# A planned kernel for a state-space convolution beside a gated feed-forward: another order of the same work

## The chip, the cores and the metric

The kernel runs on one core of a Trainium2 chip. The metric is the device time of one execution in microseconds, given as the median of several runs. A core has TensorE (PE in the profile, with its weight loads as PEld), VectorE (DVE), ScalarE (ACT), GpSimd (POOL) and SyncE (SP), and 16 DMA engines that move what the queues of SP and POOL ask for.

## The reference

```python
def reference(A_u, A_A_re, A_A_im, A_B_re, A_B_im, A_C_re, A_C_im, A_log_dt, A_Dskip, B_x, B_w_gate, B_w_up, B_w_down, gate_w):
    x = A_u                                           # 1 x 2048 x 512
    g = _sigmoid((x * gate_w).sum(-1, keepdims=True))
    a = _A_ref(x, ...)   # K[d,l] = Re sum_n C exp(dt A l) dt B, N = 128; y = causal conv of u with K (by FFT) + u * Dskip
    b = _B_ref(x, ...)   # (sigmoid(x Wgate) * (x Wup)) Wdown, F = 1792
    return g * a + (1 - g) * b
```

All arrays are float32. A is a diagonal complex state-space model per channel (512 channels, 128 states), whose kernel K of 2048 taps is convolved with the input. B is a gated feed-forward of width 1792. A gate per row mixes them.

## The kernel before, in words

**Feed-forward.** The 2048 rows are taken in two halves, each in two blocks of 512 rows; the 1792 hidden columns in 14 slices of 128, in groups of 3, 4, 4 and 3. Each float32 operand is split in a high and a low part (`split`, line 1057 on): a DMA into a staging buffer `st`, a copy on ScalarE, a subtraction on VectorE. A product is three matmuls (high-high, high-low, low-high). `hidden` (matmuls at line 1130, tile `gups`) makes gate and up products; `post` makes the gated hidden tile on ScalarE and VectorE in turn (lines 1173 to 1180); `down` (line 1202, tile `dps`) sums a group's slices for 128 rows in one accumulation bank; `add` scales it by 1 - g and adds it to the output in memory by an accumulating DMA of POOL (line 1226), or, for late rows, into a tile on VectorE (line 1215).

**State-space part.** `steps` computes exp(log_dt) on POOL, stores it (`dts`, line 446) and it is read back to all partitions by `preludes` (lines 468, 469). `powers`, `angles`, `magnitudes` and `tables` (lines 509 to 628) build tables of the powers of exp(dt A) on VectorE and ScalarE; `tables` contracts them over the 128 states on TensorE (line 653, tile `kps`, 16 blocks). `second` applies the first step of a discrete transform (line 683, `wps`, 8 blocks), evicts to `kev` and stores to memory `a_k` (line 698). `rows` does the same for the input (line 742, `ups`, 8 blocks), stored to `a_u` (line 782). `passes` works in two halves j of 256 channels, four steps each: it loads constants `wwu`, `wwk`, `wwv`, the input's part `au` (line 819) and the kernel's part `ak` (line 828); `ustep` transforms au (line 849, `s2u`), `kstep` transforms ak (line 876, `s2k`), `prod` multiplies them on VectorE, `inverse` transforms back (line 914, `ips`), `evict` copies and stores to `b_s` (line 936). `finals` reads `b_s` (line 977), `last` makes the last transform (line 990, `fps`), scales by g and adds to the output.

The matmuls of these steps are small and use the array in pieces (128x32, 32x64, 32x32, 64x32); those of the feed-forward use all of it. s2u, s2k, ips, wps and ups each need both of the two double banks `xb`; fps needs one. In the first half there is one buffer `big` for au and ak in turn; in the second there are three, two of them in space of the tables (in the profile they appear as `parts`).

**The order.** Each part is a generator that yields one step at a time (engine, cost, function, what it waits for). `Plan.run` takes the letters of the string `ORDER` one after another; a letter names a kind of step and an engine, and the first waiting step of that kind on that engine is put out. So ORDER is the program order on every engine, the DMA issues of SP and POOL among them; each engine works its instructions off in that order, and each instruction waits for its data and buffers by semaphores. The costs that steps give are used in `Plan` for times in the plan: with a given ORDER they decide only which of several equal free buffers a step takes, and no instruction. The letters that this text needs:

| letter | step | letter | step |
|---|---|---|---|
| d, e | hidden, down on PE | 5, 9, # | ustep, kstep, inverse on PE |
| Y, p, c, + | tables, second, rows, last on PE | f, $ | loads of passes, of finals, on SP |
| D, E, F | loads of x, of gate and up, of down weights | x, r, ) | stores to a_u, a_k, b_s |
| A, C, L | step sizes, pw table, prelude loads | g, 2 | late output rows (SP), accumulating DMA (POOL) |

Of the kernel before, what the change touches and what calls it, by code (L numbers as in the profile page):

```python
# [66 lines left out]
ORDER = (
    "ABEjDkhidDhEdHGDhjikddEjikIEDjkhddiEjkKZatatatdEdayzjktbFlDhiEjdyzAdkdddDhiEmedjkFydduzDhiLLMlNymMCOOPGDhdiydQOFRSdldmQE"
    "QQbZzezddQOTRyzejQWyddkWTWOWyTEjEzWdEWd0eeeTd1dOPQWEzWcWddjyyyUVVWkW0eeZdejdkvxxxW0exzvcLZx1xzWxaUeeaxzOEdUUyQWUWzFa1dWv"
    "xyQdRSTadWkExxxEyddRWtWX0YTtztQjvzTTUdtbxxxyseexeddQyyOVdVbZdUUzUUkRuj0e1leedScZQXyz0YdWzjTR1WkdseWGnovxedymWzjWeTdyddTk"  # L70
    "LTzdWkWzWWWxyzvyx1EUWEWdz0eedxFxy1xFxcedFZWjVzkWddldmWlmyyVUzUdxalmtUvxxaxx0ejvaxpqdaeeEUzyRSTdxqzje02yEtWddeeeeRTTEtWkd"
    "WWX0Y2tdrybxErTUseeededbMZzVNxMdOO02edejyeeVUPQOkUydUdQzUjRkScXZzEQz0YQQO2dTRseejQWydeneWTrjWWWWdkWdWWzvyzWxyeddzdWTv0ee"
    "eWTWdU1yEzky0eeeecdZOVVxoEWx0eeeeWzddWx2OPQdvjr2kOQQUExFUxly2UUzLRyduxSTFxkvWRmdWpxydadtzWXjkTTzFa0YlmxyTQlxFdylmUtsdzmd"
    "xeeyezadtjVxkQzxyLzeOVUExaEdj0qeUete2Uqer2r0dURyESTeeezyXed0YQb2jksR2dTbWzWedeeeTjZkckWdTy0eeWeWeWvxxxxEdUdV20eeZeexvWrx"
    "xxxWdcWVnW2WW0eejeezyWUUWUU2zWRSdyvx0eeeFFzoTdeWdRFWxlvpmrkdyzWWX2ldDDmD0YTyzTTxl2hdmiqsydehehUdMNizMOOeLxViPQOVUUUUdRSQ"
    "dx0DeQyzQXe2e0QOTRyddYQW2zWWsnodWqxrrrrOWTWyzThWOPWeedQdpWedTiWUxyWWOdqDDxWzWqrrr0edeVeyWzrVUUWUU0ddhyQDhQezdfRSf4566yzW"
    "hTRe2Wdd2e0QidyDhWeXiTieeizdy0YTTUQzfOf89%VVUUUdULdddseeQey2zX0dR%S2u2YdWyzWTRW%sndydW%WETef!EjkWFzeeTd02dTWUWyjWzWkW#&f"
    "ffdW&))))4VddVUWUEUeUWyzeeEdyzWR01e&&))))jdee01W5WfWeeSoe668pd0eeeq1TRWXq9rrEyzdyzk%r0YTT1TUdseyz%MddedV%NeMl%dOVydUjfd!"
    "#ydOPQjdOQQUUUXrzk0kQRSffEQO&YsddQeezWW1edEWWWjkEdWTRyzyjydTWnzd0eeejy&)dGW))WTzWkdzdm4)W0eeefdykWF1TUzOWEyz&dydWFoVWdVU"
    "UUjz&d)51))UOyfz668dRSlmy)lWdpWTdRkdyqqfrWdWzX90FzEY%TTTyzlyU1ddErrjkdyPmmQzseeee%Vd0e2eeeOEz%QVWUUU%!URdQ0e2eeeQXyQOdS0"  # L80
    "z2YTRQWWWWWW#fWWdjkyseeeeWdWEno&rdT&))))WTf40ee2eeTdUWj&k&5)jW)dy0ee2eedVfW))ffVd6zyWWzUU60Uep8UqEqRS2WTedeer9zdWXdRTydy"
    "0TYd%s%e%F%2!kerF#TU((dElm)z)))ydedejkrVzdVzddUUFyUlUXm0j&Y&Eyy))))jlrEdzkEkzmFsnopqqeedd$y$*jrzlmrdrrgy$f$+,*zzfydd-dy-"
    ",zfdzefy,k.z.e,3+--,ee45768g.ffef.e-,,3fE9%%%%ffgjd4d.ededj578e.,kEeyz3,E69%%%edegjff!.%fd.fed#((&ge)&)4k5376e)f)8g)E)f9"
    "yjy)z)k!f%e%edefd2%d3f#(&))&)&)d)ye4)56%e))6jfkd!8#$&&))))ee&()))$)9z3ykee%dd%%dyged%!e#&zzyg$$())))3d(())))ez*ed*+,zy-+"
    ",--zdyde-dFld$-zy--$z--F$dyd*+,dl$d*-d-yF$$--*-,+,..,elzme,..mzym$eeeeeee-z-3$3-e,33+yez,.,.e-ee,--g*--g-gee+3g,..,e-3ee"
    "-3-g--eeeee-g3ge3g")
# [243 lines left out]
def body(ctx, tc, xp, xt, prm, ldt, dsk, gw, wgu, wdn, c_wu, c_wf, c_wk, c_wwk, c_wwu, c_wwv, c_pw, out):  # L330
    nc = tc.nc
# [333 lines left out]
    def second(q, kss, kst, kready):  # L665
# [29 lines left out]
        te = []  # L695
        for x in range(4):
            dst, src = a_k[q // 4][q % 4, x], kev[32 * x:32 * x + 32]
            te.append((yield "SP", kb(215), lambda: S.dma_start(
                dst.rearrange("r l k d -> l r (k d)"), src.rearrange("p (r k) d -> p r (k d)", r=2)), [max(end)]))
# [72 lines left out]
    def urest(t4, e, i, ph, banks, tp):  # L772
        es, = yield EVU, 1
        ev = es.tile("evu")
        te = yield ("ACT", "DVE"), either(2 * D), lambda eng: copy(eng, ev, ph), [tp, es.t]
        banks.free(te)
        done = []
        for r in range(2):
            for h in range(2):
# [2 lines left out]
                done.append((yield "SP", kb(150), lambda: S.dma_start(dst, src), [te]))
# [7 lines left out]
    def passes():  # L790
# [11 lines left out]
        for j in range(NW):  # L802
# [9 lines left out]
            for p2 in range(4):  # L812
# [6 lines left out]
                ta.append((yield "SP", kb(520), lambda: S.dma_start(au.rearrange("p i g d -> p (i g d)"), src), [sa.t, rdone.t]))  # L819
# [8 lines left out]
                tk.append((yield "SP", (kb(740), 0.2), lambda: S.dma_start(ak.rearrange("p o i g d -> p o (i g d)"), src), [sk.t, kdone[j].t]))  # L828
# [34 lines left out]
    def kstep(wks, wwk, sk, ak, ready, both, tk):  # L863
# [6 lines left out]
        def mms():  # L870
            for i in range(2):
                for c in range(2):
                    for g_ in range(4):
                        for r in range(2):
                            q = slice(64 * r, 64 * r + 64)
                            mm(pk[i][32 * g_:32 * g_ + 32, r, c], wwk[q, i, g_, c], ak[q, :, i, g_], start=True, stop=True,  # L876
                               tile_position=(64 * r, 32 * g_), skip_group_check=True)
# [177 lines left out]
    def split(kind, src, hi, lo, slot, ready, n=512):  # L1055
# [4 lines left out]
        t = yield "SP", kb(0.55 * n), lambda: S.dma_start(flat if len(src.shape) == 2 else st, src), [s.t]  # L1060
# [239 lines left out]
```

## Time and profile before

| | |
|---|---|
| median of 3 runs | 615.53 us (615.13 to 615.72) |
| the profiled execution | 617.09 us, of which the span of instructions 615.3 us |
| TensorE clock granted, mean | 0.983 |
| instructions | 16787 |
| matmuls | 7147: 1344 `gups`, 672 `dps`, the rest pieced blocks |
| moved by DMA | 104.19 MB, mean 169 GB/s |

A row of busy time by line names the line, the engine, the operation, what is written and read, the shape and the count, then busy us, mean ns of one, idle time ahead and what ended it. Consecutive matmuls overlap, so the mean of one is longer than the step from one to the next. A row of the timeline has start, duration, engine, line, what is written and read, and the count of instructions merged. A row of PE's waits has us in total, times and the longest. A load's time to landing runs from its issue to its last byte.

### The profile page before, as it was taken

The page shows a single profiled execution, that of the slowest core. Times are in us where ns is not written, and L with a number is a line of the kernel's source. Part 1 is how long each engine was busy: PE and PEld are TensorE (multiplying, and loading weights), DVE is VectorE, ACT ScalarE, POOL GpSimd, SP SyncE. Part 2 cuts the span into 40 slices and gives each one's busy share as a digit, 9 for nine tenths or more (in the row PEclk, how much of TensorE's full clock was granted, in tenths as well). Part 3 has the DMA queues.
Part 4 walks back from the last instruction along what each step waited for, and adds up shares of the span by engine and source line. Part 5 has one row for each costly group of instructions (what it writes and reads, how often), then busy time and mean ns, then how long its engine had stood idle before and what let it go on. Part 6 is the DMA issues. An engine that isn't in the chain of part 4 may idle for free.

```text
span 615.3 us, 16787 instructions
## 1 busy us (share of the span) xinstructions
PE 590.5 (96%) x7147; PEld 453.0 (74%) x7147; DVE 539.9 (88%) x765; ACT 414.8 (67%) x663; POOL 51.2 (8%) x80
## 2 busy tenths in 40 slices
PE   7999999999999999996999999999999988998997
PEld 3777777887778777884787778777777756676775
DVE  3899999999999997996899999999988566867897
ACT  3597979688798767995867878788957432231340
POOL 5000000010101111100110000001110022000031
PEclk7999999999999999997999999999999998999999
DMA  7612807562675586487518725444955799898776
GB/s 224 216 34 74 289 26 215 176 134 35 172 177 142 109 183 154 82 191 221 126 19 242 201 80 167 135 152 54 244 146 137 220 300 315 245 271 264 236 200 164
DMA packets 74156, 104.19 MB, mean 169 GB/s; under 512 B 7009, under 2 KB 45793, under 8 KB 73058
## 3 DMA queue, kind: packets, MB, share of 16 engines
q1 hardware_dynamic: 67170, 92.64, 49.9%
q0 software_dynamic: 6912, 10.49, 12.5%
q8 instruction: 56, 0.92, 0.6%
q14 instruction: 18, 0.15, 0.1%
HBM read 61.15 MB, written 41.95 MB: 168 GB/s over the span
## 4 chain that ended last, share of the span: by engine, by line
PE 75%; DMA 9%; issue 7%; DVE 3%; ACT 2%; SPq 1%; POOL 0%; DVEq 0%; ACTq 0%; POOLq 0%
PE gups L1130 40%; PE dps L1202 20%; PE kps L653 5%; PE s2k L876 3%; DMA ak<-a_k 2%; PE wps L683 2%; PE s2u L849 2%; PE ips L914 2%; PE ups L742 1%; DMA b_s<-ev 1%; DMA out<-part 1%; DMA st<-xt 1%; PE fps L990 1%; DMA wwk<-c_wwk 1%; DMA st<-wdn 1%
## 5 line engine op out<-in xcount | busy, mean ns | idle before, releaser
L1130 PE MATMUL gups<-x,gu 128*128 128x512 f32 x1344 | 334.7, 397 | 2.7 <-ACT x L1063 1.5
L1130 PEld LDWEIGHTS gups<-x,gu 128*128 128x128 f32 x1344 | 252.4, 190 | 69.6 <-issue 9.2
L1202 PE MATMUL dps<-dnw,h 128*128 128x512 f32 x672 | 172.7, 395 | 0.9 <-DVE h L1180 0.9
L1202 PEld LDWEIGHTS dps<-dnw,h 128*128 128x128 f32 x672 | 124.5, 188 | 36.9 <-issue 7.1
L1226 POOL DMA_DIRECT2D out<-part x32 | 28.3, 885 | 421.4 <-ACT part L1221 286.4
L581 ACT ACTIVATE B<-B 128x32 f32<-128x32 f32 (+2 forms) x96 | 53.9, 676 | 0.3
L1221 ACT ACTIVATE part<-dps,omg 128x512 f32<-128x512 f32 x48 | 32.8, 682 | 27.6 <-PE dps L1202 26.9
L1175 DVE SCALAR_TENSOR_TENSOR sg<-sg,gups 128x512 f32<-128x512 f32 x56 | 37.8, 680 | 9.8 <-ACT sg L1173 5.9
L1173 ACT ACTIVATE sg<-gups 128x512 f32<-128x512 f32 x56 | 33.0, 590 | 14.7 <-PE gups L1130 13.7
L1179 ACT ACTIVATE h<-sg 128x512 fp32r<-128x512 f32 x56 | 34.6, 622 | 11.3 <-DVE sg L1175 11.3
L609 DVE TENSOR_TENSOR t<-T,bz 128x1024 f32<-128x1024 f32 (+3 forms) x48 | 41.2, 859 | 0.6
L611 DVE TENSOR_TENSOR T<-T,t 128x1024 f32<-128x1024 f32 (+3 forms) x48 | 41.4, 863 | 0.3
L610 DVE TENSOR_TENSOR T<-T,bz 128x1024 f32<-128x1024 f32 (+3 forms) x48 | 41.3, 861 | 0.0
L1180 DVE TENSOR_TENSOR h<-sg,h 128x512 fp32r<-128x512 f32 x56 | 38.2, 685 | 2.5 <-ACT h L1179 2.4
L1064 DVE TENSOR_TENSOR gu<-st,gu 128x512 fp32r<-128x512 f32 (+1 forms) x50 | 32.9, 663 | 7.0 <-ACT gu L1063 7.0
L1063 ACT ACTIVATE gu<-st 128x512 fp32r<-128x512 f32 (+1 forms) x50 | 30.3, 607 | 12.0 <-DMA st<-wgu 11.9
L653 PEld LDWEIGHTS kps<-B,T 128*32 128x32 f32 x2048 | 29.9, 110 | 9.3 <-issue 6.7
L653 PE MATMUL kps<-B,T 128*32 128x64 f32 x2048 | 33.0, 220 | 2.1 <-issue 2.1
L355 ACT ACTIVATE ev<-ips 128x512 f32<-128x512 f32 x23 | 13.0, 594 | 30.9 <-PE ips L914 17.1
L499 ACT ACT_TABLE_LOAD x21 | 26.9, 1283 | 0.3
L692 ACT ACTIVATE kev<-wps 128x1024 f32<-128x1024 f32 x16 | 15.8, 1024 | 13.5 <-PE wps L683 13.3
L575 DVE TENSOR_TENSOR B<-pp,pw 128x1024 f32<-128x1024 f32 x16 | 19.6, 1224 | 4.9 <-PE kps L653 4.8
(124 smaller groups left out, 698.6 us busy)
## 6 DMA issues: line engine op xcount, KB each, us to landing
st<-wgu SPq DMA_DIRECT2D x46, 256.0 KB, 4.7
a_u<-evu SPq DMA_DIRECT2D x64, 128.0 KB, 3.8
a_k<-kev SPq DMA_DIRECT2D x32, 256.0 KB, 3.7
out<-part POOLq DMA_DIRECT2D x32, 256.0 KB, 4.7
b_s<-ev SPq DMA_DIRECT2D x64, 128.0 KB, 3.1
st<-wdn SPq DMA_DIRECT2D x25, 256.0 KB, 3.8
ak<-a_k SPq DMA_DIRECT2D x5, 1024.0 KB, 7.1
parts<-b_s SPq DMA_DIRECT2D x10, 512.0 KB, 6.1
```

The costliest lines, as they stand in the source:

```text
L581: A.activation(B[:, :, 0, 1 << k::2 << k], B[:, :, 0, 1:64 >> k:2], AF.Exp, scale=float(1 << k))
L609: yield "DVE", c, lambda: V.tensor_tensor(t2, src, sb, op=OP.mult), [t, slot.t]
L610: te = yield "DVE", c, lambda: V.tensor_tensor(dst, src, br, op=OP.mult), [t]
L611: te = yield "DVE", c, lambda: V.tensor_tensor(dst, dst, t2[:, :, ::-1], op=OP.add), [te]
L653: mm(p[32 * jj:32 * jj + 32, s], T[:, 32 * i + ch, c], B[:, ch, c], start=(c == 0), stop=(c == 1), tile_position=(0, 32 * jj), skip_group_ ...
L1064: te = yield "DVE", dve(n), lambda: V.tensor_tensor(lo, st, hi.bitcast(F32), op=OP.subtract), [te]
L1130: mm(p, gu[:, a, k, dc], x[:, b, dc], start=(dc + n == 0), stop=(dc == NC - 1 and n == 2))
L1173: t = yield "ACT", actp(512), lambda: A.activation(sg, pg_, AF.Tanh, scale=0.5), [tg, ss.t]
L1175: t = yield "DVE", dve(512), lambda: V.scalar_tensor_tensor(sg, sg, 1.0, pu, op0=OP.add, op1=OP.mult), [t, tu]
L1179: t = yield "ACT", act(512), lambda: A.activation(h[:, 0], sg, AF.Copy), [t, hs.t]
L1180: t = yield "DVE", dve(512), lambda: V.tensor_tensor(h[:, 1], sg, h[:, 0].bitcast(F32), op=OP.subtract), [t]
L1202: mm(p, h[:, a, 128 * s:128 * s + 128], dn[:, b], start=(f == fs[0] and n == 0), stop=(f == fs[-1] and n == 2))
```

## The change

The string ORDER is replaced by another of the same 2178 letters' length. The count of each letter is the same but for four kinds: evictions of the inverse on ScalarE 23 to 20 and on VectorE 9 to 12, steps of `last` on ScalarE 22 to 23 and on VectorE 34 to 33 (steps that may run on either). Beside it, cost figures that the planner uses are edited: TensorE's cost of a change of array shape, and the sizes that stand for the rate of single transfers. No instruction's shape or operand is edited.

```diff
 ORDER = (
-    "ABEjDkhidDhEdHGDhjikddEjikIEDjkhddiEjkKZatatatdEdayzjktbFlDhiEjdyzAdkdddDhiEmedjkFydduzDhiLLMlNymMCOOPGDhdiydQOFRSdldmQE"
...
+    "kABEjDkhiddEjkEjDkhiHIEjDhGiddddKZEjatDhiddatkddEjkatatbEyddDjkhEDyddjzkddhizAyuFlyzDhmizdiDhLLidydeMNzdddGyFMyddCOOPlmQ"
...
-            c = n + (0.0 if mode == self.last else 0.09 if self.last == "f" else 0.21 if mode == "f" else 0.1)
+            c = n + (0.0 if mode == self.last else 0.18 if self.last == "f" else 0.33 if mode == "f" else 0.2)
...
-        t = yield "PE", ("f", 0.95, 4), lambda: mm(p[:, 0], warm[:1, :P], row, start=True, stop=True), [t, bank.t]
+        t = yield "PE", ("f", 1.95, 4), lambda: mm(p[:, 0], warm[:1, :P], row, start=True, stop=True), [t, bank.t]
...
-            te.append((yield "SP", kb(215), lambda: S.dma_start(       # a_k
+            te.append((yield "SP", kb(295), lambda: S.dma_start(
...
-                ta.append((yield "SP", kb(520), lambda: S.dma_start(au...
+                ta.append((yield "SP", kb(1010), lambda: S.dma_start(au...
...
-                tk.append((yield "SP", (kb(740), 0.2), lambda: S.dma_start(ak...
+                tk.append((yield "SP", (kb(1130), 0.2), lambda: S.dma_start(ak...
```

The other edits are of the same kind: stores to a_u and b_s 150 to 139, s2k 1.57 to 1.68 us, loads of b_s 540 to 485, accumulating stores 215 to 230, staging loads 0.55 to 0.52 per column.

The PE letters of the two strings, from the first c on, around the places that the prediction speaks of (p is the fourth and the eighth, 5 and 9 the first and the fifth; the last row is from the fifth 5 to the last #):

```
before  p e d d e d e e d d e d 5          after  p d e d e d d d e d d e e d e 5
before  p e e d d d + d d d d e e + e e 5 e e 9
after   p d d d d d d d d d + + d d d e 5 d e e 9
before  5ee9ddeded5ee9ededed#e5e9eededd#de5ed#ee9eedddede#
after   5dee9edeeded59eededed#eeee59ededee#eed5ee#d9deeededd#
```

And the SP letters around the first load of a_u (x is the last of its 64, r the last four of the first 16, f the loads of passes):

```
before  D D x r r r r D f f D f f
after   D D r x r r r f f f D D f
```

From the first of the loads of passes in the second half on, the SP letters are (g late output rows):

```
before  f $ f f f g f f f f E f f g E E g f f f f g ) ) ) f ) g ) E ) f ) )
after   f f f f g f f f f f f g E f f f f g ) ) f ) ) E ) f f g E ) ) ) f f
```

More of the change, by code (lines that the diff above doesn't have):

```diff
@@ L72 @@
[L72 to L83, printed above, removed]
@@ L84 @@
-    "yjy)z)k!f%e%edefd2%d3f#(&))&)&)d)ye4)56%e))6jfkd!8#$&&))))ee&()))$)9z3ykee%dd%%dyged%!e#&zzyg$$())))3d(())))ez*ed*+,zy-+"
-    ",--zdyde-dFld$-zy--$z--F$dyd*+,dl$d*-d-yF$$--*-,+,..,elzme,..mzym$eeeeeee-z-3$3-e,33+yez,.,.e-ee,--g*--g-gee+3g,..,e-3ee"
-    "-3-g--eeeee-g3ge3g")
+    "kABEjkDhiddEjkEjDkhiHIEjDhGiddddKZEjatDhiddatkddEjkatatbEyddDjkhEDyddjzkddhizAyuFlyzDhmizdiDhLLidydeMNzdddGyFMyddCOOPlmQ"
+    "OQzRSzeddEbZQTQRQOjkQWEEFlcZmeyTyEdWWzWdzWdjkWOTWyOEWPF0eeeyTvxxxxWzWdU1EjkvxxxxWQddyWzW0ee1eddcOWWzVWQWdVUWUdUEUElyjkWj"
@@ new lines @@
+    "RyvxxxSk0e1ZeXaatxaeddazjQyjvxxxxGjQd01YTRdyseeezddtztTddTzkTUkdtEQObVyVUUULdUu0ee1yzbyzRSeZXd0dyQYcWWjseedeWvxxZdzddWzd"
+    "WTRdWykmzyvWnWydxTTT0eeFWxEFxzlWkcdyZaledWWUVzVddxdWLmFmWzx1ExWa0yUzUljmeyvxxeetkzUdxWUxWRSeEa02aydvxxxxee1opejedTqdWtRW"
+    "Xy02YTdzdtTEktbseedeTUebMqdVNEzMOO02dVUeeedeyZPQOjkyUjyddQUUXrRzQ0Y2QckSZr1QOseeeezTznddREjvxxrxQWxWWWryydd0eeee2TzzdWTW"
+    "WkWWdTOvxxWWUEyxWzOcxPW0eyzeee2WWdVyVU0dedFdevFQUjkydUZal2xxOQaEazEjQWkdtyeeddvURSxFoxTQpzddjzRTWkWjWXkTamxxExF0Yd2yzyTz"
@@ new lines @@
+    "tUQylmseezOdldmeVlmyzVe0deeeExeUQuUUUEXRyt0dzSjY2k2dTERtWWbWbZseWWqeeneqrTWrrrjW0deTjeedyzcZ2TvxxxLkxUWWe0WdWeedeevcxWWy"
+    "xVk2zxVd0eeeexUU2UURSjkvxxyxvop0eeeeqWdTRyz0eeeFlFzdedLxddxDxWmFTlWmWTWyT2WDX0YDyzzhiDhiyhdsedeqlrhrUzMNmedViMLOOPQiddOV"
+    "UU2Ur0eeeUXQyQd0QzxrR2QOdSYyzTedRseenQWWopdOWWOWWy2zTTWPWW0e2dedTdDdUdeyqqzW2VDrxWWWrydrzQOrfff4dVUUUDhiyzQ0eedeQDyUWzW0"
+    "yhRSWW56fTedheeddRWhdQi6WiTzX80Yyzi9TdTUy22dsezQV%%VUUUUXOdyzee0ydQRSdY2sWd%eee0dyneefWTEWj%!#WEFdzjWkRWl2fde&dWzWdd&))E"
@@ new lines @@
+    "))fWkTWTmW0TUW4Eoedyzj&&)yde5VkzWWW)VUULUf)y1UeWzdu0e16yzedRSe6p0feedeE8jykEWdqT12RWWXqr9r0YdzTddTT%ydUjjV%MNsdeVEjeeyd%"
+    "dz)MOOUPQOyfdedQyUQUURXd10Y%Q!#rfQOSTRsde1eQE&Wz&TWf4WnzdzWdkWTyWdWzW))TU0eeedWyzkr)1ydzdVWOdyWVWUU)&&5E)of0edefUjUkFk6y"
+    "F)6)1zpq)8WRWSTWddydREq9rzWWTjkWOfdeWldzdlXPmd%T0YQOjyzyrzydzdmQTUFdyseeeEzlme%V02VQdee1Qkee02Qjy%dU%!UUeUkRSeeXOEze0dYT"
+    "RQWWW2#seeEyjfzWkWdedWWnWW&&))))TyTWdWf4TUW&e0WrdEezedoW&)))5)fjreeVWVUUUU60eeeWy6pRjqqeWdSWTyRf89%%W%d20eTeeedX2T0Y2TUs"
@@ new lines @@
+    "%dy#df!Vkze&zG2EredVydeedkrFlr())U)y)UUUX0YF(dEr&)))mj)lskzemnopEjkFdFE$zyq$*qrlddyzrddjrzydkdyddzzr$mz$*+,-gf+,-,,f4-yz"
+    "dfddeyzy5f..,,lgzy668fmzfdee39-,,%%%f4efjdfeedeyfgd..573%kE.689%.,,.%efedededy!f4.%#3ee&e%(zefy(jf(g576893ez))kf%de!)%%)"
+    "dE)jkeffe4g3E)#()e&e)fdf()))jf)(k%57e!)6e)zy))#E8(gdgy$&)2())&)$9)j3kdee)e)d%)ed%dy%g$$%!#*z&()))d&z)dy())))3eeeFe*zFz+y"
+    "F3+,zlld-dy--d$,d--me$-d-$*+,---dy-dd--$*l$-+$*,,zy$+$*.med.,me,,dzzeee--y3eee.yee,ezze.,+e-yz.3e-3.,,-3-g.--gg-g,-3-eee"
@@ L88 @@
+    "3--.eg--gee3geee3g")
 XLATE = 0
@@ L781, in urest @@
                 src = ev[64 * r + 32 * h:64 * r + 32 * h + 32].rearrange("p j (w d) -> p (j w) d", w=NW)
-                done.append((yield "SP", kb(150), lambda: S.dma_start(dst, src), [te]))
+                done.append((yield "SP", kb(139), lambda: S.dma_start(dst, src), [te]))
         es.free(max(done))
@@ L818, in passes @@
                 src = a_u.rearrange("r s e j w g d -> w (r s e j) g d")[j][:, 8 * p2:8 * p2 + 8].rearrange("x g d -> x (g d)")
-                ta.append((yield "SP", kb(520), lambda: S.dma_start(au.rearrange("p i g d -> p (i g d)"), src), [sa.t, rdone.t]))
+                ta.append((yield "SP", kb(1010), lambda: S.dma_start(au.rearrange("p i g d -> p (i g d)"), src), [sa.t, rdone.t]))
                 ready, both = [Ev(), None], Ev(2)
@@ L827, in passes @@
                 src = a_k[j].rearrange("o x r l (c p y) d -> p (r l c) (o x) (y d)", c=2, p=4)[p2]
-                tk.append((yield "SP", (kb(740), 0.2), lambda: S.dma_start(ak.rearrange("p o i g d -> p o (i g d)"), src), [sk.t, kdone[j].t]))
+                tk.append((yield "SP", (kb(1130), 0.2), lambda: S.dma_start(ak.rearrange("p o i g d -> p o (i g d)"), src), [sk.t, kdone[j].t]))
                 plan.spawn(kstep(wks, wwk, sk, ak, ready, both, max(tk)), "kstep")
@@ L877, in mms @@
                                tile_position=(64 * r, 32 * g_), skip_group_check=True)
-        t = yield "PE", ("64x32", 1.57, 129), mms, [tk] + [b.t for b in banks]
+        t = yield "PE", ("64x32", 1.68, 129), mms, [tk] + [b.t for b in banks]
         sk.free(t)
@@ L935, in evict @@
                 src = ev[64 * r + 32 * c:64 * r + 32 * c + 32]
-                end.append((yield "SP", kb(150), lambda: S.dma_start(dst, src), [max(te)]))
+                end.append((yield "SP", kb(139), lambda: S.dma_start(dst, src), [max(te)]))
         es.free(max(end))
@@ L976, in finals @@
                 src = b_s[j][:, :, q, 4 * t4:4 * t4 + 4].rearrange("c k j d -> (c k) (j d)")
-                tb.append((yield "SP", kb(540), lambda: S.dma_start(b[:, q].rearrange("p j d -> p (j d)"), src), [sb.t, bdone[j].t]))
+                tb.append((yield "SP", kb(485), lambda: S.dma_start(b[:, q].rearrange("p j d -> p (j d)"), src), [sb.t, bdone[j].t]))
             plan.spawn(last(j, t4, b, sb, max(tb)), "last")
@@ L1022, in last @@
                 t = 4 * t4 + k[i]
-                done.append((yield "POOL", kb(215), lambda: nc.gpsimd.dma_start(out[t, :, cols], y[:, i], accum_op=OP.add), [max(t1), begun[t]]))
+                done.append((yield "POOL", kb(230), lambda: nc.gpsimd.dma_start(out[t, :, cols], y[:, i], accum_op=OP.add), [max(t1), begun[t]]))
                 begun[t].set(done[i])
@@ L1059, in split @@
         st = flat if len(hi.shape) == 2 else flat.rearrange("p (a b) -> p a b", a=hi.shape[1])
-        t = yield "SP", kb(0.55 * n), lambda: S.dma_start(flat if len(src.shape) == 2 else st, src), [s.t]
+        t = yield "SP", kb(0.52 * n), lambda: S.dma_start(flat if len(src.shape) == 2 else st, src), [s.t]
         def halves():
```

3 lines of the change are left out of this document (removed).

## The prediction

> **What bounds the kernel now.** I read the page's engine totals first, then busy time by stage, then PE's waits and, where those lie, the timelines of PE and SP and the chain of waits.
>
> ```profile
> span 615.3 us, 16787 instructions
> ```
> ```profile
> PE 590.5 (96%) x7147; PEld 453.0 (74%) x7147; DVE 539.9 (88%) x765; ACT 414.8 (67%) x663; POOL 51.2 (8%) x80
> ```
> ```profile
> 20.00:60.00 40.00, 38.75 (x195) 30.33 (x194) 39.86 (x70) 30.93 (x54) 0.00 (x0) 1.00 0.30 90
> 260.00:300.00 40.00, 34.64 (x466) 27.32 (x458) 32.92 (x46) 30.71 (x47) 3.48 (x4) 0.91 0.76 189
> 500.00:540.00 40.00, 35.98 (x567) 24.02 (x566) 30.36 (x36) 9.60 (x16) 6.62 (x8) 0.96 0.99 279
> ```
>
> The span is 96% TensorE. The stage rows (busy us of PE, PEld, DVE, ACT, POOL, then PE clock, DMA share, GB/s) say where it isn't: 260 to 300 and 500 to 540 lose over 5 and over 4 us of PE and are the rows with a lowered clock. VectorE is a second pacer: 39.86 of 40 us busy in 20 to 60, but only 32.92 in 260 to 300, when TensorE stands still.
>
> ```profile
> PE s2u L849 <- DMA wwk<-c_wwk: 5.4, 1, 5.4
> PE s2k L876 <- DMA ak<-a_k: 2.6, 1, 2.6
> PE kps L653 <- issue: 2.1, 3, 1.4
> PE s2k L876 <- ACT ev L355: 1.7, 1, 1.7
> ```
>
> Two waits for loads of intermediate results stand out. "Issue" waits have no releaser in the trace; a new order can't be shown to remove them, so I leave them in. With the operations unchanged, the new order can only change PE's idle time, the array's changes of shape, and clock lost by idling.
>
> **One: fewer changes of shape.** The PE letters of ORDER, read off, give the sequence of PE steps: 517 in both. The letters d and e use the whole array; Y, p, c, 5, 9, #, + use it in pieces. Changes of shape fall from 121 to 114, stretches of pieced work between whole-array work from 58 to 53.
>
> ```profile
> 565.90 1.36 PE gups L1130 x6
> 567.94 1.43 PE ips L914 x61
> 569.37 1.59 PE gups L1130 x6
> ```
>
> Six whole-array matmuls take 1.36 us (0.227 each), and 1.59 right behind a pieced block. One stretch less so saves about 0.23: five save 1.2 us (ends 0 and 2, if entering a block costs something too).
>
> **Two: the first load of a_u.** SP issues in order.
>
> ```profile
> 268.29 0.44 SPq L782 DMA_DIRECT2D a_u<-evu  x1
> 270.96 2.77 SPq L698 DMA_DIRECT2D a_k<-kev  x4
> 273.83 1.50 SPq L1060 DMA_DIRECT2D st<-xt  x1
> 275.51 1.56 SPq L815 DMA_DIRECT2D wwu<-c_wwu  x1
> 277.13 0.44 SPq L819 DMA_DIRECT2D au<-a_u  x1
> ```
> ```profile
> 266.46 2.10 PE L683 MATMUL wps<-wk,kst 32*64 32x128 f32 x128
> ...
> 285.72 2.37 PE L849 MATMUL s2u<-au,wwu 32*32 32x256 f32 x64 [5.36 <-DMA wwk<-c_wwk]
> ...
> 289.47 2.90 PE L1130 MATMUL gups<-x,gu 128*128 128x512 f32 x8
> ```
> ```profile
> a_u<-evu SPq DMA_DIRECT2D x64, 128.0 KB, 3.8
> ...
> au<-a_u SPq DMA_DIRECT2D x4, 1024.0 KB, 7.2
> ```
>
> PE's clock is the time base. The wps block (letter p, its fourth) starts at 266.46; PE is free for s2u at 285.72 - 5.36 = 280.36, 13.9 us later; the au load, issued 277.13, keeps s2u waiting until 285.72, 19.3 us after wps. (The row names the wwk load, which s2u does not read; of its own inputs au is the late one.) Then 5.36 us of idling cost clock too: eight gups take 2.90 where 8 x 0.227 is 1.8, and the three dps ahead of them are slow alike. With s2u itself slow (2.37, against 1.43 for the ips block of the same shape and count above) the place costs about 5.4 + 0.9 + 1.1 = 7.4 us by these rows, and with 0.5 for the dps 7.9.
>
> In the new order, between the same two blocks stand 9 d and 6 e instead of 6 d and 5 e: 9 x 1.36 + 6 x 0.68 against 6 x 1.36 + 5 x 0.68, so 16.3 against 11.6, 4.8 us more cover; PE reaches s2u 18.7 us after wps. The load's side: SP can issue the first of the four a_k stores 4.5 us after wps (270.96 - 266.46), and the last a_u store now stands behind that one (before, it was ahead, at 268.29): 4.9. It must have landed before au is issued: with the median 3.8 that is 8.7, and with 7.2 for au the data is there at 16, or at 18 if each runs a microsecond over its median. The load of xt that sat ahead of wwu (1.50 us) now comes after. So 18.7 against 16 to 18: no wait, at best by 0.7 us. Bounds: all 7.9 gone, or, if SP gets to that store 5 us late, none. I take 7.0.
>
> What is late next is VectorE.
>
> ```profile
> 70.86 1.21 DVE L611 TENSOR_TENSOR T<-T,t 128x1024 f32<-128x1024 f32 x1
> ```
> ```profile
> 72.75 1.44 PE L653 MATMUL kps<-B,T 128*32 128x64 f32 x88
> ```
> ```profile
> 477.44 1.22 DVE L590 TENSOR_TENSOR B<-B,ex 128x1024 f32<-128x1024 f32 x1
> ```
> ```profile
> 479.27 1.94 PE L653 MATMUL kps<-B,T 128*32 128x64 f32 x124
> ```
>
> These are the first and the last of 16 kps blocks; each starts about 0.6 us after VectorE's last operation on its tables, and 14 of the 16 within 2.3 us. So TensorE can't run ahead of VectorE by more than that, unless VectorE too is freed of idle time. It idles 40 - 32.92 = 7.1 us in the stage of this wait; part of that was waiting on the stalled PE. I give back 2 us (between 0 and 7): net -5.
>
> **Three: the first a_k load of the second half.**
>
> ```profile
> 482.85 1.34 PE wps L683 x77
> 489.75 4.75 DMA a_k<-kev
> 495.41 13.73 DMA ak<-a_k
> 509.27 3.21 PE s2k L876 x64
> ```
>
> From the last wps block to this s2k the data needs 509.14 - 482.85 = 26.3 us: stores, then a load of 13.73 us in a crowd. Between them the order had 7 d and 8 e, and has 13 d and 3 e: 13 x 1.36 + 3 x 0.68 = 19.7 against 15.0, 4.7 more. The wait was 2.6, and the s2k group took 3.21 where the one quoted under part four takes 1.96, so 3.9 together; the stage's clock of 0.96 leaves some 0.4 for the gups behind it. Cover of 4.7 takes it all: -4.3 (ends 0 and -5.2). [...]
>
> **Four: s2u and s2k back to back.** Twice the new order puts 9 directly behind 5; before, at least one e lay between.
>
> ```profile
> 534.01 2.01 PE L849 MATMUL s2u<-parts,wwu 32*32 32x256 f32 x64 [0.54 <-ACT ev L355]
> 535.95 0.96 PE L1202 MATMUL dps<-dnw,h 128*128 128x512 f32 x3
> 537.16 1.96 PE L876 MATMUL s2k<-parts,wwk 64*32 64x256 f32 x64 [0.25 <-ACT parts L355]
> ```
>
> s2k needs both banks that s2u filled. With one e (0.7) between, it still idled 0.25, so without it about 1.0 each: +2.0 in all (0.5 to 3). The wait of 0.54 of this s2u for the inverse's eviction has four e ahead of it now, not one, and goes, with the 0.25: -0.8. Net +1.2.
>
> **The rest at nothing.** The fourth s2u of the first half keeps its cover (4 d and 8 e behind the inverse, now 5 d and 6 e: 10.9 both). So does the last s2k (two e, now one d, 1.36 both): its 1.7 stays. Further loads of the first half have 7.5 us of PE work (the fourth s2u to its s2k: 1 d, 6 e and a wps of 2.1) or more, against a median of 7.2 (au's; ak is of the same size). If one is late, it costs what it lacks, a microsecond or so. The tail after the last fps has two e more and nothing that lands late. Three evictions go from ScalarE to VectorE, late, where neither is full (30.36 and 9.60 of 40 in 500 to 540). The edited costs are the planner's figures and add no instruction.
>
> Sum: -1.2 - 5.0 - 4.3 + 1.2 = -9.3. The profiled execution took 617.09 (span 615.3 and 1.8 around it); the median is 615.53, so I subtract from the median: **606.2 us**.
>
> **The rivals.** *The crowd stays.* In 500 to 540 the DMA engines are 0.99 busy. If the loads are late because the engines are full, an earlier place in the queue only lets another be late: part three gives nothing and part two half: -1.2 - 2.5 + 1.2 = -2.5, so 613.0. [...] Against it: the first wait falls in a stage of 0.76, and the third's cover grows in PE time, whatever the queue.
>
> *Slower: SP's queue sticks.* Every load of the second half goes through SP, in order.
>
> ```profile
> 495.41 1.13 SPq L828 DMA_DIRECT2D ak<-a_k  x1
> 496.58 8.33 SPq L954 DMA_DIRECT2D parts<-out  x1
> ...
> 509.15 7.02 SPq L832 DMA_DIRECT2D wwv<-c_wwv  x1
> ```
>
> Two issues that usually take 0.4 us took 8.33 and 7.02 there; behind the first stood the next step's loads, behind the second late rows and weights. PE lost little, since its own loads were out. The new order keeps the pattern (loads of four, then a late output row) and brings the loads of the third step forward, into the same crowd. If SP sticks once ahead of a load that PE then waits for, up to 8.3 comes back: 614.5. If it does so twice, 15.4: 621.6, with lost clock more. It decides against the change when over 9.3 us of sticking lies ahead of loads that are needed. For it: 0.99 of the engines busy. Against it: the store of a_k that these loads wait for is out 4.7 us earlier in PE's time.
>
> *No change:* VectorE gives back all 7 of part two and the s2k moves with it, so that only parts one and four remain: 615.5.
>
> **How the numbers follow.** A measurement of this kernel can tell 0.2% (1.2 us) from nothing. Forecast 0.60 (all of it faster), crowd 0.14 (faster), no change 0.08, SP sticking past its point 0.18. So faster 0.74, same 0.08, slower 0.18. The low end takes parts one to three at their ends and four at its least: -2 - 7.9 - 5.2 - 0.3 is 600. The high end reaches past one sticking, to 617.
>
> **What would show it.** Right: PE's wait at the first s2u under 1.5 us and no half clock near 285; no wait at the s2k behind the last wps; about 1 us ahead of two s2k; VectorE over 36 us busy in 260 to 300. Wrong: s2u or s2k waiting behind an SP issue of 7 us or more (SP sticking); kps waiting for VectorE (no change); ak still 13 us in flight and s2k waiting (crowd); or waits of PE at places that had none, which I priced at nothing.

## The result and the profile after

| | before | after |
|---|---|---|
| median of four runs, us | 615.33 (613.40 to 615.72) | 598.01 (597.14 to 600.63) |
| profiled execution: time / span, us | 617.09 / 615.3 | 597.14 / 595.4 |

The ratio is 0.973, with a 95% interval of 0.969 to 0.977: the change gains 17.3 us. The direction was forecast, the size was not: 9.3 us were forecast, and 598.0 lies below the range's low end of 600. By the two profiled executions the difference is 19.9 us, since the one of before lies 1.8 us above its median and the one of after 0.9 below. (A fourth run of the kernel before moves its median from the prediction's 615.53 to 615.33.)

The page's totals after the change, and the same three stages by window (busy us of PE, PEld, DVE, ACT, POOL, then PE clock, DMA share, GB/s):

```profile
span 595.4 us, 16804 instructions
...
PE 584.0 (98%) x7147; PEld 451.0 (76%) x7147; DVE 542.2 (91%) x767; ACT 412.9 (69%) x661; POOL 51.2 (9%) x80
```
```profile
20.00:60.00 40.00, 40.00 (x205) 32.20 (x204) 38.24 (x66) 31.48 (x55) 0.00 (x0) 1.00 0.42 129
260.00:300.00 40.00, 40.00 (x527) 31.95 (x526) 39.38 (x49) 33.49 (x53) 3.73 (x5) 1.00 0.61 154
500.00:540.00 40.00, 37.52 (x666) 25.60 (x637) 32.72 (x42) 10.91 (x17) 2.68 (x3) 1.00 0.90 248
```

The stage 260 to 300 has no gap in PE any more and no lowered clock (1.00; in the trace of before 0.50 was granted from 285 to 291), and VectorE works 39.38 of 40 us in it (32.92 before). The list of PE's waits has lost the two loads at its top, and also the kps blocks' "issue" wait of 2.1; the last s2k's wait of 1.7 is missing too. The two back-to-back pairs are new, and so is one wait of a dps for ScalarE:

```profile
PE s2k L876 <- ACT parts L355: 2.3, 2, 1.1
...
PE dps L1202 <- ACT part L1221: 1.1, 1, 1.1
```

PE's timeline shows both places of the prediction, from the wps block to the block that used to wait, neither with a wait now. SP's timeline shows the stores and loads between the same blocks:

```profile
260.67 2.10 PE L683 MATMUL wps<-wk,kst 32*64 32x128 f32 x128
...
279.27 1.50 PE L849 MATMUL s2u<-au,wwu 32*32 32x256 f32 x64
...
464.51 2.10 PE L683 MATMUL wps<-wk,kst 32*64 32x128 f32 x128
466.53 12.56 PE L1130 MATMUL gups<-x,gu 128*128 128x512 f32 x54
479.02 1.09 PE L990 MATMUL fps<-b_in,wf 64*32 64x256 f32 x32
...
485.93 1.50 PE L849 MATMUL s2u<-parts,wwu 32*32 32x256 f32 x64
...
490.31 1.96 PE L876 MATMUL s2k<-ak,wwk 64*32 64x256 f32 x64
```
```profile
266.02 0.33 SPq L698 DMA_DIRECT2D a_k<-kev  x1
266.40 0.42 SPq L782 DMA_DIRECT2D a_u<-evu  x1
...
270.40 1.13 SPq L819 DMA_DIRECT2D au<-a_u  x1
...
471.41 2.64 SPq L977 DMA_DIRECT2D parts<-b_s  x2
...
475.56 0.33 SPq L819 DMA_DIRECT2D parts<-a_u  x1
...
480.21 0.38 SPq L828 DMA_DIRECT2D ak<-a_k  x1
...
487.91 6.92 SPq L832 DMA_DIRECT2D wwv<-c_wwv  x1
```

The first s2u starts 18.6 us after its wps block (18.7 forecast), and its load was issued 9.7 us after that block and was there 5.8 us later, 15.5 in all (16 forecast). (The row of letters for the changed order, ahead of the prediction, shows one d too few between these blocks. The string has 9 d and 6 e there, as the prediction counts, and the trace 54 gups and 18 dps.) The s2k of the second half comes 25.8 us after its wps block; its load took 7.4 us (13.7 before) and landed 2.7 us ahead of it. SP still sticks, here for 6.92 us at 487.91, and no load that PE waited for lay behind it.

To see where all 19.9 us went I measured, for each stretch of pieced blocks, the time from the start of the last whole-array matmul before it to the start of the first one behind it, and took away 0.227 and the blocks' undisturbed lengths in these traces (s2u and ips 1.52, s2k 1.98, kps 2.02, wps 2.12, fps 1.12). What is left is lost time:

| place | lost before | lost after | change | forecast |
|---|---|---|---|---|
| first s2u and the slow matmuls behind it | 7.9 | 0 | -7.9 | -7.0 and 2.0 given back |
| first s2u and s2k of the second half | 5.1 | 0 | -5.1 | -4.3 |
| the two s2u-s2k pairs | 1.5 | 2.6 | +1.1 | +1.2 |
| all small remainders (shape changes) | | | -1.4 | -1.2 |
| fourth s2u of the first half | 1.6 | 0 | -1.6 | 0 |
| waits at kps, wps, and kps with ips, nearly all "issue" | 4.6 | 1.3 | -3.4 | 0 |
| last s2k and the ips ahead of it | 1.8 | 0.8 | -1.0 | 0 |
| waits of whole-array matmuls; first block; start and tail | | | -0.9 | 0 |

The column of changes sums to -20.2 with its roundings. The four costed parts were forecast at -9.3 and measured -13.3; the places put at nothing brought another 6.9. Each column is one execution: by the medians the change is 17.3, so some 2.6 us of the sum belong to these two executions and not to the change.

### The profile page after: what moved, and what is told of

Same layout as the page of the kernel before. It is cut to its first block, busy times and chain, and to the rows that moved or that the text cites. A ratio compares the mean times of both kernels' runs of the same rounds, so it can differ in the third digit from the quotient of the medians.

```text
span 595.4 us, 16804 instructions
## 1 busy us (share of the span) xinstructions
PE 584.0 (98%) x7147; PEld 451.0 (76%) x7147; DVE 542.2 (91%) x767; ACT 412.9 (69%) x661; POOL 51.2 (9%) x80
## 4 chain that ended last, share of the span: by engine, by line
PE 89%; DVE 3%; DMA 3%; SPq 2%; ACT 1%; issue 1%; DVEq 0%
PE gups L1130 50%; PE dps L1202 24%; PE kps L653 5%; PE wps L683 3%; PE s2k L876 2%; PE ups L742 1%; DMA b_s<-ev 1%; PE fps L990 1%; PE s2u L849 1%; PE ips L914 1%; SPq L936 1%; DVE tt L889 1%; DMA parts<-out 1%; DMA st<-xt 1%; DVE uf L890 0%
## 5 line engine op out<-in xcount | busy, mean ns | idle before, releaser
L1221 ACT ACTIVATE part<-dps,omg 128x512 f32<-128x512 f32 x48 | 32.8, 683 | 27.4 <-PE dps L1202 25.7
L1173 ACT ACTIVATE sg<-gups 128x512 f32<-128x512 f32 x56 | 33.1, 590 | 21.1 <-PE gups L1130 20.2
L355 ACT ACTIVATE ev<-ips 128x512 f32<-128x512 f32 x20 | 11.3, 596 | 18.8 <-PE ips L914 11.1
L586 DVE TENSOR_TENSOR B<-B,ex 128x1024 f32<-128x1024 f32 x16 | 19.6, 1223 | 3.1 <-ACT B L581 2.8
```

What stands on the lines that cost most here:

```text
L1173: t = yield "ACT", actp(512), lambda: A.activation(sg, pg_, AF.Tanh, scale=0.5), [tg, ss.t]
```

## The experiments

Theory one is the prediction's: each load has its own time, and a wait is what the PE work ahead of it lacks (cover). Its rivals are the crowd (the load is late because the DMA engines are full, whatever stands ahead), VectorE as the pacer that takes gains back, and the stages acting as one chain. All ratios are against the kernel before, run on the same chip; only letters of ORDER differ.

**The first s2u, moved alone in the old order.**

```diff
-...RSf4566yzWhTRe2Wdd2e0QidyDh...
+...RSf466yzWhTRe2Wdd2e0Qid5yDh...
-...WeXiTieeizdy0YTTUQzfOf89%VVUUUdULddd...
+...WeXiTieeizdy0YTTUQzfOf8%VVUUUdULddd9...
```

> The kernel before, with only one pair of steps moved: the first s2u of the first half stands two e and three d later (2 x 0.68 + 3 x 1.36 = 5.4 us of TensorE work that other steps need anyway), and the s2k behind it four d later, so that it stays as far behind its s2u. Theory one (cover: the load has its own time, and the wait is what the work ahead of it lacks): the wait of 5.4 us and the halved clock behind it go, about 7.9 us by the trace of before, VectorE gives nothing back, and the run is about 607.5 us. Theory two (the prediction's: VectorE had idled with the stalled TensorE and is late afterwards): about 5 or 6 of the 7.9 come back as a gain, 609.5 to 610.5, with kps blocks waiting for VectorE behind it. Theory three (crowd): the load lands later too, and the run is within 1.2 us of before.

Measured: 608.97 us, ratio 0.986 (0.983 to 0.990): faster by 7.1 us by the medians, by 8.4 (6.3 to 10.4) by the ratio. PE's timeline, its list of waits, and the stages:

```profile
282.75 1.49 PE L849 MATMUL s2u<-au,wwu 32*32 32x256 f32 x64
```
```profile
PE kps L653 <- ACT part L1221: 1.5, 1, 1.5
...
PE gups L1130 <- ACT sg L1173: 0.9, 1, 0.9
...
PE gups L1130 <- DVE sg L1175: 0.4, 1, 0.4
```
```profile
260.00:300.00 40.00, 38.52 (x519) 30.38 (x518) 35.96 (x47) 34.48 (x55) 3.49 (x4) 1.00 0.79 207
300.00:340.00 40.00, 38.73 (x575) 29.31 (x574) 39.79 (x52) 29.23 (x45) 1.76 (x2) 1.00 0.57 150
```

The wait and the lowered clock are gone: too little cover was the cause of both, and the crowd is refuted here (the load still took 7.2 us, 7.9 before). But in this trace not all of it stays. At 289 a kps block waits 1.5 us for the ScalarE eviction (L1221) that had the PSUM bank, and at 315 to 319 gups wait 0.9 and 0.4 us for the gate's ScalarE and VectorE steps, with VectorE busy 39.79 of 40 us in that stage. That is some 3 us given back in this one execution, more than the 2 us of the prediction: moved alone, the step runs into VectorE's and ScalarE's pace. It would leave a gain of 5, and the ratio gives 6.3 to 10.4. The same execution also lost 1.7 us less at the first s2k of the second half than the trace of before and 1.2 less in the first block, places that the edit doesn't touch; so how much a move of this kind gives back over many executions is not shown.

**The same s2u, moved the other way in the new order.**

```diff
-...zQOrfff4dVUUUDhiyzQ0eedeQDyUWzW0yhRSWW56f...
+...zQOrfff45dVUUUDhiyzQ0eedeQDyUWzW0yhRSWW6f...
```

> The changed kernel, with only the first s2u of the first half moved earlier by about 4.8 us of TensorE work (to the distance behind the wps block that it had before the change). In the changed kernel its load landed 3.1 us before the s2u. Theory one (cover): a wait of about 1.7 us comes back, without a halved clock since it is short: plus 1.5 to 2, so 599.5 to 600. Theory three (crowd or queue: the load is early now whatever the cover): no wait, within 1.2 us of the changed kernel.

Measured: ratio 0.978 (0.974 to 0.981), 602.94 us. PE's timeline:

```profile
275.37 1.49 PE L849 MATMUL s2u<-au,wwu 32*32 32x256 f32 x64 [2.95 <-issue]
```

The wait is back, 2.95 us (1.7 forecast), and the row names no releaser, though the load landed only 0.6 us before the block's start. In four traces (the kernel before, this one, and the first two splices below) this s2u starts 0.6 to 0.7 us behind the landing of its load, whatever the row names: the load is what it waits for. These 0.6 us, and a load of 6.3 us instead of 5.8, are most of what the forecast lacked. So cover is needed as well as enough. No lost clock shows: the s2u took 1.49, as in the changed kernel (1.50). In the trace of before, too, the granted clock was 1.00 in and behind waits of 1.35, 1.39 and 1.73 us. The ratio is 0.004 (2.6 us) over that of the changed order's repeat below; the intervals just overlap.

**The first s2k of the second half, moved alone in the old order.**

```diff
-...-,,3fE9%%%%ffgjd4d.ededj578e...
+...-,,3fE%%%%ffgjd4d.eded9j578e...
```

> The kernel before, with only the first s2k of the second half (the one that waits 2.6 us for its load of 13.7 us) moved behind four d and two e more (4 x 1.36 + 2 x 0.68 = 6.8 us). Theory one (cover): the wait and the slow clock around it go; what the trace of before loses there is 0.75 at the s2u and 3.95 at the s2k with 0.36 behind, and the s2k's 3.95 to 4.3 go: about 611.3 us. Theory two (crowd, the DMA engines being 0.99 busy): the load lands later by as much, or the next one does, and the run is within 1.2 us of before.

Measured: slower, ratio 1.010 (1.006 to 1.015), median 622.93 us of five executions; a sixth took 2004.83 us, is not explained, and is left out. PE's timeline:

```profile
515.53 0.96 PE L1202 MATMUL dps<-dnw,h 128*128 128x512 f32 x3 [1.23 <-DVE parts L1215]
...
519.84 1.96 PE L876 MATMUL s2k<-ak,wwk 64*32 64x256 f32 x64
523.68 0.62 PE L849 MATMUL s2u<-parts,wwu 32*32 32x256 f32 x4 [1.89 <-issue]
527.76 2.34 PE L849 MATMUL s2u<-parts,wwu 32*32 32x256 f32 x60 [3.46 <-DVE uf L890]
```

The s2k itself waits for nothing and takes 1.96, as cover had it. But the next s2u, now right behind it, waits till 527.76: it needs the PSUM banks that hold the s2k's result until VectorE has taken it (four operations L889 and L890 of 1.23 us, and two sums between them). From s2k to that s2u 7.9 us pass, and VectorE's operations alone fill all but 1.4 of them. Neither theory had this: a block that is moved alone shortens the stretch behind it. The dps ahead of them wait 1.23 us for VectorE, which waits for a load of `out` that SP's queue had held for 7.80 us: here the sticking queue does cost PE time. Cover ahead of a block has to come from work that no other block needs as its own cover.

**The same place, moved the other way in the new order.**

```diff
-...,-,,f4-yzdfddeyzy5f..,,lgzy668fmzfdee39-...
+...,-,,f45-yzdfd6689deyzyf..,,lgzyfmzfdee3-...
```

> The changed kernel, with the first s2u of the second half moved ahead of the three d and one e before it (4.8 us), and the s2k behind it ahead of one d, one e and one e more, so that it stands about 5.5 us nearer to the last wps block, as before the change. In the trace of the changed kernel its load landed 2.7 us before the s2k. Theory one (cover: the load has its own time): a wait of about 3 us in all comes back at the s2u and the s2k, and slow matmuls behind it: plus 3 to 4. Theory two (crowd: the load is quick in the new order whatever stands ahead of it): within 1.2 us of the changed kernel.

In the kernel as it ran, the s2k moved by 2.7 us, not 5.5, and the s2u by 4.8. Measured: ratio 0.982 (0.979 to 0.984), 603.52 us: 5 us of the gain lost. PE's timeline:

```profile
482.85 0.62 PE L849 MATMUL s2u<-parts,wwu 32*32 32x256 f32 x4 [1.93 <-DVE yt L1007]
484.88 2.34 PE L849 MATMUL s2u<-parts,wwu 32*32 32x256 f32 x60 [1.41 <-DVE mn L1002]
```

Most of the price lies at the s2u: two waits, 1.93 and 1.41 us, and slow matmuls behind them (the next 18 gups take 4.86 us, 4.42 in the changed kernel). Its load landed at 482.6, and VectorE had drained the fps results that precede it (L1002, L1007) by 484.9. The s2k had no wait, and its load took 7.5 us (7.4 in the changed kernel): here the load's speed did not hang on where PE stood. So neither theory is tested at the s2k. The prediction spoke of the s2k alone; the new order had to keep the s2u off two more things at this place.

**Old and new order, spliced.** Three kernels take one order up to a letter and the other's order for what is left behind it. The first two are joined at the first letter f, which issues the first s2u's loads (on SP at 275.5 us in the trace of before, 269.4 after; on PE, in the old order, directly ahead of that s2u), the third behind the last wps block.

```diff
-ORDER = (changed order)
+ORDER = (changed order to the first f, then the old order of the rest)
```

> The changed order up to the start of the second half's first fps steps, and the old order of what is left behind it. By the two traces the first part holds the first s2u (7.9), the fourth s2u (1.55), the 'issue' waits (some 4) and the change of VectorE's share; the second holds the first s2k (5.1) and little else. Theory one (the stages add up): 12 to 14 us of the 17.3 stay, 602 to 604. Theory two (the gain is one chain: an early start in the first half is what relieves the second): nearly all stays, 598 to 600, or, if the old second half waits for what the new first half has put off, little, 608 and over.

Measured: 611.52 us, ratio 0.992 (0.989 to 0.995). The orders are joined earlier than this expectation says, so its sum of stages doesn't apply; the next expectation starts from that. The first s2u has 7 d and 3 e behind its wps block, 11.6 us as in the old order, and its wait is back:

```profile
276.26 2.37 PE L849 MATMUL s2u<-au,wwu 32*32 32x256 f32 x64 [3.20 <-DMA wwk<-c_wwk]
```

```diff
-ORDER = (old order)
+ORDER = (old order to the first f, then the changed order of the rest)
```

> The old order up to the issue of the first s2u's loads (about 265 us), and the changed order of what is left behind it: the other half of the run before, whose cut lay at this same place and not, as its expectation says, at the second half. That run kept 3.7 of 17 us and a wait of 4.2 at the first s2u. Theory one (the stages add up): 12 to 14 us are gained here, 601 to 603.5, with no wait at the first s2u. Theory two (one chain: an early start of the first part relieves what follows): under 9, over 606.

Measured: 601.95 us, ratio 0.975 (0.970 to 0.980), as theory one had it, but for a small wait that is left:

```profile
282.20 1.48 PE L849 MATMUL s2u<-au,wwu 32*32 32x256 f32 x64 [0.82 <-DMA st<-xt]
```

By the ratios the two splices gain 5 and 15 us, each give or take 2 to 3, by the medians 3.7 and 13.8, together 17.5, against 16.3 of the whole order's repeat below: within the noise the stages add up, and most of the gain hangs on the order from the first s2u on.

```diff
-ORDER = (old order)
+ORDER = (old order to the last wps, then the changed order of the rest)
```

> The old order up to the last wps block (482.8 us in the trace of before), and the changed order of what is left behind it. By the two traces this last part holds 5.4 us (the first s2u and s2k of the second half 5.1, the last s2k 1.8, less the two back-to-back pairs). Theory one (cover and stages): about 5 us gained, 609.5 to 611, the first ak load in 7 to 9 us. Theory two (crowd: the load is slow because of what the first part has put off, and the new order of the last part alone does not help): ak in 12 us or more, and within 1.2 us of before.

Measured: 616.56 us, ratio 1.003 (0.999 to 1.007): nothing is gained. PE's timeline, and SP's:

```profile
499.21 0.69 PE L990 MATMUL fps<-parts,wf 64*32 64x256 f32 x16 [3.26 <-DMA parts<-b_s]
500.48 1.11 PE L990 MATMUL fps<-parts,wf 64*32 64x256 f32 x16 [0.58 <-DMA parts<-b_s]
...
508.84 1.49 PE L849 MATMUL s2u<-au,wwu 32*32 32x256 f32 x64
```
```profile
493.32 2.33 SPq L977 DMA_DIRECT2D parts<-b_s  x2
...
496.72 0.60 SPq L819 DMA_DIRECT2D au<-a_u  x1
...
497.90 0.39 SPq L828 DMA_DIRECT2D parts<-a_k  x1
```

The s2u and s2k have no wait here either, but the second fps block does, 3.84 us: the new order puts it directly behind the first one, and the load of b_s isn't there. Between the last wps block and the fps block PE had only 4 d and one e to do; in the changed kernel it has 9 d (the 54 matmuls of 12.56 us above). The old order had spent the other d earlier. Counting letters, d at 1.36 and e at 0.68, the work ahead of the last wps block is 378.1 us in the old order and 372.0 in the new one: 6 us are saved up for the end. And the a_k load took 12.8 us, as in the old order, 4.6 us behind the b_s loads; in the changed kernel it is issued 8.8 us behind them and takes 7.4. The prediction's crowd has its right here: the load's speed seems to depend on what is in flight with it. Which neighbour it is was not tried by itself. The b_s loads, 512 KB each, are one candidate. The a_u load of the same step is another, itself 1 MB: it is issued 0.8 us ahead of the a_k load in the kernel before, 1.2 here, and 4.7 in the changed kernel. In the changed kernel's own trace a later a_k load, issued at 503.3 us, 1.7 us behind an a_u load and 30 us behind the last b_s load, took 11.6 us, so b_s loads are not needed for a slow one.

**Two small waits, moved in the old order.**

```diff
-...WX2ldDDmD0YTyzTTxl2hdmiqsydehehUdM...
+...WX2ldDDmD0TyzTTxl2hdmiqsydYehehUdM...
```

and the fourth s2u of the first half (5) one d later.

> The kernel before, with two single blocks moved, far from each other: the kps block that follows a wps block after 5 us and loses 1.65 us to an 'issue' wait stands two d (2.7 us) later, and the fourth s2u of the first half, which loses 1.55 us, one d (1.36 us) later. Theory one (an 'issue' wait comes of blocks of many small matmuls that follow each other too soon, and the s2u's of its load): both waits go, by 1.3 to 1.65 and about 1.4, and the run is 2.7 to 3 us faster. Theory two (both places wait for something that moves with the work): the same waits stand at the new places, and the run is within 1.2 us of before.

Measured: 614.11 us, ratio 0.999 (0.996 to 1.001). The kps block in PE's timeline before, and then with the two blocks moved:

```profile
241.48 1.76 PE L653 MATMUL kps<-B,T 128*32 128x64 f32 x108
244.59 0.53 PE L653 MATMUL kps<-B,T 128*32 128x64 f32 x20 [1.35 <-issue]
```
```profile
244.18 1.99 PE L653 MATMUL kps<-B,T 128*32 128x64 f32 x128
246.89 1.65 PE L1202 MATMUL dps<-dnw,h 128*128 128x512 f32 x6 [0.72 <-ACT kst L661]
...
254.77 2.37 PE L1202 MATMUL dps<-dnw,h 128*128 128x512 f32 x9 [1.47 <-ACT part L1221]
```

The kps block runs its 128 matmuls in one piece; before, it broke off after 108 of them for 1.35 us of "issue". So such a wait can be removed by order, which the prediction denied itself. A count of PE's matmuls in program order says more. In all traces the "issue" waits of kps and wps blocks stand behind one of the same six matmuls, the 986th, 1753rd, 2391st, 3791st, 4556th or 5702nd. These are nearly whole multiples of 128 apart: from 2391 to 3791 it is 11 times 128 less 8. So the place is one in PE's stream of instructions, and the order decides whether it is felt. Where it was, the last 128 matmuls had passed in 2.9 to 6.3 us (with the moved block, 7.3), though other such places were run through; what PE waits for there is not shown. But the gain is given back at once: dps wait 0.72 us for the kps result's eviction (L661), which is now later, and 1.47 us for the next (L1221). At the fourth s2u 1.0 of 1.6 us is left, with a load of 8.5 us (8.2 before). Both theories were too simple: the waits go, and their neighbours take them over.

**The pairs, taken apart in the new order.**

```diff
-...fgd..573%kE.689%.,,.%efedededy!f4...(jf(g576893ez))kf%de!)...
+...fgd..573%kE.68%.,,.%efe9dededy!f4...(jf(g57683ez))kf%de9!)...
```

> The changed kernel, with its two back-to-back pairs of s2u and s2k taken apart: the second step's s2k two e later, the third's one d and two e later. In the trace of the changed kernel s2k idles 1.47 and 1.13 there (the evictions of the s2u's second bank). Theory one (the pair's wait is the eviction's time, and anything between hides it): minus 2.0 to 2.6, less up to 0.9 if one of the places adds changes of the array's shape: 595.5 to 597. Theory two (whatever is gained is given back at the next wait, the ips blocks waiting for ScalarE): within 0.7 us of the changed kernel.

Measured: ratio 0.976 (0.973 to 0.979), 602.30 us, against 0.973 for the changed order's repeat: no gain, rather a loss of 1.7 us by the ratios, whose intervals overlap. In its trace the next ips block also waits 2.2 us for VectorE's products (L890). PE's timeline, and two windows:

```profile
502.16 2.87 PE L1202 MATMUL dps<-dnw,h 128*128 128x512 f32 x6 [1.94 <-DVE parts L1215]
...
520.80 0.96 PE L1202 MATMUL dps<-dnw,h 128*128 128x512 f32 x3 [1.94 <-DVE parts L1215]
```
```profile
500.00:504.00 4.00, 2.06 (x19) 1.47 (x6) 3.74 (x5) 1.82 (x3) 1.89 (x3) 0.78 0.41 98
...
518.00:522.00 4.00, 2.06 (x50) 1.22 (x35) 3.08 (x4) 1.66 (x2) 0.00 (x0) 1.00 0.83 222
```

The e steps put between the pair wait themselves, 1.94 us twice, since VectorE takes their predecessor's result (L1215) only behind the s2u's: its own order still has it so, and it sits idle 1.60 us until the s2u's result is there. It is theory two with another engine: VectorE, not ScalarE, holds the gain back, and the filling itself pays first. Moving PE's letters alone leaves the other engines in an order made for the old place.

**The edited figures.**

```diff
-ORDER and planner figures of before
+ORDER of the changed kernel, planner figures of before
```

> The changed order of work with the old planner figures left in: if the edited figures add no instruction and move none, this is the changed kernel again, and serves as its repeat on this chip. Theory one (only the order counts): 0.973 of before, 597 to 600. Theory two (the edited figures do something by themselves): away from that by more than 1.2 us.

Measured: 598.94 us, ratio 0.973 (0.971 to 0.976): the order is the whole change. In the two traces the sequence of PE's, VectorE's, ScalarE's, GpSimd's and SyncE's operations is the same. From PE's list of waits:

```profile
PE s2k L876 <- ACT ev L355: 1.8, 1, 1.8
```

The last s2k's wait, which the profile after had lost, is back in this repeat of the same instructions: the 1.8 us that vanished there were that execution's. With the ips block ahead of it, 2.8 us are lost at that place here, 0.8 in the profile after and 1.8 before.

## Why the prediction fell short

The direction was right, and so was cover as the mechanism at the first s2u. Two steps failed: the 2 us given back in part two, and the rest put at nothing. Part three came out near its size in part by luck.

**Part two.** The cover was right to 0.1 us; the load's arrival was right to half a microsecond, by two errors that offset (it was issued 1.0 us later than the sum has it and took 1.4 less). The 7.9 us all went. What failed is "I give back 2 us (between 0 and 7)". With the one step moved alone about 3 us came back in its trace. In the whole new order nothing did, and VectorE idles far less there. The same long window in both traces, first before and then after:

```profile
20.00:460.00 440.00, 429.88 (x5192) 339.46 (x5191) 415.39 (x584) 352.87 (x557) 26.23 (x30) 0.99 0.56 144
```
```profile
20.00:460.00 440.00, 438.17 (x5417) 346.40 (x5416) 427.71 (x595) 362.63 (x574) 27.13 (x31) 1.00 0.58 148
```

VectorE idles 24.6 us there before (440 - 415.39) and 12.3 after. More than half of the difference, 6.5 us, lies in the stage of the wait itself, 260 to 300 (7.1 before, 0.6 after); 2.6 lie ahead of it and 3.3 behind. That PE can't run ahead "unless VectorE too is freed of idle time" was the prediction's own condition, and it came true where the prediction had looked: it took part of the 7.1 us for lasting, and nearly all of it went. With the step moved alone 4.0 us of idle time stay in that stage. The splice of old and then new order tells that the part ahead isn't needed: VectorE idles as long as before from 20 to 260 us there (10.3 against 10.5), and from the s2u to 340 us PE waits for neither VectorE nor ScalarE. That VectorE's order behind the s2u is the cause is argued from these traces; no run changes it alone.

**Part three** gained 5.1 where 4.3 was forecast, but not by 4.7 us of cover. PE reached the s2k only 1.9 us later behind its wps block than before (25.8 against 23.9 without the wait): d and e took 4.7 more, but the "issue" waits of 1.08 and 0.60 us in that stretch and some changes of shape were gone. The load came 3.2 us sooner (23.1 against 26.3), which the prediction didn't forecast, and without it a wait of some 0.7 us would have stayed. The fps blocks and the s2u ahead had to be kept whole as well; the late splice shows that the last part's order alone gains nothing.

**"The rest at nothing"** failed as a step. "The fourth s2u of the first half keeps its cover" was true, and the wait went all the same: its load is issued 8.1 us ahead of the s2u now, where 7.1 lay between the issue and the time PE was free before, for a load of 8.2. By the two timelines of SP a staging load and a store to a_k, 1.1 us together, stood ahead of it before and stand behind it now; that this is the reason wasn't tried. Of the "issue" waits it said that "a new order can't be shown to remove them", and 3.4 us of waits went, nearly all of this kind; the kps block moved alone shows that order can do it, but only together with what stands around it. That "its 1.7 stays" holds on the whole: the wait is gone in one execution and back in the repeat, so the -1.0 of its row in the table is that execution's and not the order's.

**Parts one and four** were right: -1.4 against -1.2, and +1.1 against +1.2. Part four's two terms were both low and offset: the new pairs cost 2.6 (2.0 forecast) and the old waits there 1.5 (0.8).

**The low end** of 600 summed the bounds of the costed parts alone. The waits in the trace that had no part of their own, some 8 us (4.6 of kps and wps, 1.6 of the fourth s2u, 1.8 of the last s2k), had no bound below zero in it. Half of them would have brought the low end to 596.

**The rivals.** SP sticks as before (6.92 us), and in the changed kernel it costs nothing. The crowd is refuted at the first s2u. In the second half the a_k load's 12.8 or 7.4 us go with what was issued just ahead of it, and the gain there hangs on that as much as on cover.

## What to carry to other kernels

Filling work is a budget: a block moved alone mostly hands its wait to its neighbour (of the four single moves meant to gain, three gained nothing or lost), while an order laid out as a whole can pay most waits. Part of that is to save filling work for the stretch that has the long transfers, and part, as the pairs suggest, to move the other engines' steps along with PE's. When an order is changed throughout, bound every wait of the old trace below zero, the unnamed ones too, and ask how much of a second engine's idle time in the stage of a wait is only the wait's own. Before a block is moved, follow its PSUM banks: who drains them, how long that takes (7.9 us from the s2k moved alone to the s2u behind it), and which block needs them next.

## What was not expected of the hardware

- Two waits of the same 1.94 us stand in one trace (the pairs taken apart): the clock granted in the 4 us around the first was 0.78, and the matmuls behind it were slow; around the second it was 1.00. At the first s2u a wait of 2.95 us cost no clock, and one of 3.20 (the first splice) did: the s2u took 1.49 and 2.37 us. The length of a wait alone doesn't decide. In the trace of before, the 2.63 us ahead of the first s2k of the second half did cost clock: 0.73 was granted from 508 to 512 and 0.84 from 512 to 516, and the s2k took 3.21 us, 1.96 in the changed kernel. What else decides is not shown.
- The five loads of ak, 1 MB each, took between 5.4 and 13.7 us in the one trace of before. That its neighbours in flight set this is argued from the issue times.
- Within a kps block of 128 matmuls PE stopped for 1.35 us after the 108th with no releaser in the trace, and ran through when the block stood 2.7 us later. Such stops of kps and wps blocks fall at fixed places in PE's stream of matmuls, nearly multiples of 128 apart; five traces have one behind the 2391st.
